# Attention and two mixture stages on one core: the steps of the heads issued in parts by engine, 79 of the parts placed by a table, and the sums and scales of the values kept in another PSUM bank

## Chip, cores and metric

The program runs on one core of one Trainium2 chip. The metric is the time of one execution on the device in microseconds (us). The profiled execution has a span, from the first to the last instruction, and a time of its own that also holds what lies around the span.

## What is computed

An attention over 2 batches of 8 heads (768 positions, head size 64), in which a query sees the keys that have the same signs under a random projection; its output goes through a dense layer pair and then through a layer pair chosen by token.

```python
mask = q_bucket[:, :, :, None] == k_bucket[:, :, None, :]
scores = np.where(mask, scale * np.matmul(q, k.transpose(0, 1, 3, 2)), -1000000000.0)
...
attn = attn / (np.sum(attn, axis=-1, keepdims=True) + 1e-09)
x = np.matmul(attn, v)              # then rows of 512 for 1536 tokens
x = (s * np.maximum(x @ w_in, 0) ** 2 + b) @ w_out
out[mask_e] = gate * (np.maximum(x[mask_e] @ w1[e], 0) @ w2[e])   # e: the token's expert, 8 of them
```

## The kernel before

The attention takes heads 0 to 15 in pairs p. Its work is a list of events, each with a key of 10 times a block number plus a priority; a program sorts the list by key and then calls the events one after the other. A call issues all of an event's instructions, so the key sets the order on every engine at once, and each engine works through its own instructions in that order. Block 6h+j belongs to head h and key block j (768 keys are 6 blocks of 128). Events of the start have negative keys.

The events of a head are these. `trans` (L193) turns q or k of a pair on TensorE and splits it in a high and a low part: `qh`, `kh` on ScalarE, `ql`, `kl` on VectorE. `bits` (L252 to L277) multiplies both with the projection, six pairs of matmuls into one PSUM tile, and VectorE writes the signs (`aux`). `asm` and `asm_aux` copy the parts by DMA into the operands `Q1`, `Q2`, `K1`, `K2` of a head. `maxp` (L383) multiplies for one block of queries; VectorE reduces the rows to the maximum (`mx`). `mops` (L394) makes four small VectorE operands of it, and `mrow` (L407, L416) puts them into a row of `Q1` by way of TensorE and ScalarE (`NM` is written last). `st` (L429) multiplies keys with queries, ScalarE takes the exponential `e` and for most blocks its half-precision part `eh`, and GpSimd makes the rest `el`. `avs` (L451) multiplies `e`, or `eh` and `el`, with the values, for half of the queries at a time, and `fin` (L478) divides.

The values are made ready beside that: `load_v` (a DMA from GpSimd's queue), `vabs` (ScalarE, a bound of their size), `vred` (GpSimd, sums over blocks, three additions `vt`, `vsm`, `vsm`), `vscan` (column sums by TensorE), `vscale0` to `vscale2` (a common scale for a group of pairs: VectorE, a transposition by TensorE, five tiny VectorE steps, a broadcast by TensorE, a copy `sc`), `vsums` (ScalarE `vr`, `vp`, then VectorE `vb`), `vxs`, `vx`, `vxl` (values scaled and split) and `vsel` (GpSimd `VS`). There are three such groups: pair 0, pairs 1 to 3, pairs 4 to 7.

PSUM has three tiles of two banks for everything of `trans`, `bits`, `maxp`, `mrow`, `st`, `xt` and, before the change, also for `vscale1`, `vscale2` and `vscan` of the later groups (`self.ps`, tag S). Who needs a tile waits on the engine that read its last content. Two more banks, `av0` and `av1`, hold the sums of `avs` for even and odd heads. `warm` issues matmuls on zeros in the start. Heads 0 to 3 have their `maxp` inside the blocks of the heads before.

Of the kernel before, what the change touches and what calls it, by code (L numbers as in the profile page):

```python
# [20 lines left out]
HALF = 384  # L21
# [7 lines left out]
XN = [[f"x{g}{i}" for i in "hl"] for g in range(3)]  # L29
AT = dict(vx=-2, tq=-20, tk=-19, bits=-17, mo=-6, mr=2, xt=21, mx=-12, vs=4,  # L30
# [11 lines left out]
class Attn:  # L42
    def __init__(self, ctx, natctx, hlctx, qkctx, qkctx2, tc, psS, psA, ident, identb, q, k, v, proj, xt, x1, x2):
# [55 lines left out]
        self.vps = {}  # L99

# [93 lines left out]
    def trans(self, p, nm):  # L194
        nc = self.nc
        a = self.qt[p][nm]
        ps = self.ps("trans")
        for j in range(NB):
            nc.tensor.matmul(out=ps[:, j // 3, (j % 3) * 128:(j % 3) * 128 + 128], lhsT=a[:, j].rearrange("p h d -> p (h d)"), rhs=self.ident,
                             is_transpose=True)  # L200
        hl = self.hl if p % 2 else self.hl0
        hi = hl.tile([128, S], F32R, tag=nm + "h", name=nm + "h")
        lo = hl.tile([128, S], F32R, tag=nm + "l", name=nm + "l")
        nc.scalar.activation(out=h2(hi), in_=ps[:, :, 0:HALF], func=ACTF.Copy)
        nc.vector.tensor_tensor(out=h2(lo), in0=ps[:, :, 0:HALF], in1=h2(f(hi)), op=ALU.subtract)
        self.qt[p][nm + "h"] = hi
        self.qt[p][nm + "l"] = lo

    def asm(self, h, nm, parts=(0, 1)):
        p, r = divmod(h, 2)  # L210
        t = self.qt[p]
        rows = slice(64 * r, 64 * r + 64)
        i = h % 4
        dma = lambda out, in_: self.nc.sync.dma_start(out=f(out), in_=f(in_))
        hi, lo = t[nm + "h"][rows], t[nm + "l"][rows]
        if nm == "q":
            if 0 in parts:
# [34 lines left out]
    def bits(self, p):  # L252
        self.bits1(p)
        self.bits2(p)

    def bits1(self, p):
# [7 lines left out]
        t["bps"] = ps  # L264

    def bits2(self, p):
        nc = self.nc
        t = self.qt[p]
        ps = t.pop("bps")
        if p == 0:  # L270
            for o, out, m in ((32, self.Q1[1], 1.0), (96, self.K1[1], -PEN)):
                nc.vector.tensor_scalar(out=h2(out[64:76]), in0=ps[o:o + 12, :, 0:HALF], scalar1=self.thr[o:o + 12, 0:1], scalar2=m,
                                        op0=ALU.is_gt, op1=ALU.mult)
            return
        aux = (self.hl if p % 2 else self.hl0).tile([128, S], F32R, tag="aux", name="aux")
        nc.vector.tensor_scalar(out=h2(aux), in0=ps[:, :, 0:HALF], scalar1=self.thr[:, 0:1], scalar2=self.thr[:, 1:2],
                                op0=ALU.is_gt, op1=ALU.mult)  # L277
        t["aux"] = aux

    def bits0(self, nm):  # L280
# [16 lines left out]
    def vred(self, p):  # L297
# [4 lines left out]
        add(x, vn[:, :, 0:3], vn[:, :, 3:6])  # L302
        add(o, x[:, :, 0], x[:, :, 1])
        add(o, o, x[:, :, 2])

    def vscan(self, lo, hi):

        nc = self.nc
        if lo:
            self.vps = self.ps("vsum")[:, 0]  # L310
            for p in range(lo, hi):
                nc.tensor.matmul(out=self.vps[0:12, (p % 4) * 128:(p % 4) * 128 + 128].rearrange("p (h d) -> p h d", h=2),
                                 lhsT=self.one[:, 0:12], rhs=self.vsm[:, p % 4])
            return
        self.vps = self.psA.tile([128, 512], F32, tag="av1", name="vsum")
        for j in range(NB):
            nc.tensor.matmul(out=self.vps[0:12, 0:128].rearrange("p (h d) -> p h d", h=2), lhsT=self.one[:, 0:12], rhs=self.vn[0][:, :, j],
# [9 lines left out]
    def vscale0(self, i):  # L327
        self.vsr = self.sm.tile([128, 4], F32, tag="vr", name="vr", bufs=1)
        self.nc.vector.tensor_reduce(out=self.vsr[:, 3:4], in_=self.vm[:, (0, 1, 4)[i]:(1, 4, 8)[i]], axis=AX.X, op=ALU.max)
# [13 lines left out]
    def vscale2(self, i):  # L343
        ps = self.ps("vscale")[:, 0]
        self.nc.tensor.matmul(out=ps[:, 0:3], lhsT=self.one[0:1], rhs=self.vsr[0:1, 0:3])
        self.nc.vector.tensor_copy(self.sc[i], ps[:, 0:3])

    def vsums(self, lo, hi):
# [34 lines left out]
    def maxp(self, h, j):  # L383
# [23 lines left out]
    def mrow0(self, h):  # L407
# [4 lines left out]
        nc.tensor.matmul(out=ps[:, 0, HALF:512], lhsT=self.MP[h % 2], rhs=self.identb)  # L412
        nc.scalar.activation(out=h2(self.Q1[h][96:98]), in_=ps[96:98, :, 0:HALF], func=ACTF.Copy)
        nc.scalar.activation(out=self.NM[h % 3][0:12], in_=ps[0:12, 0, HALF:512], func=ACTF.Copy)

    def mrow(self, h):  # L416
        if h < 4:
            return self.mrow0(h)
# [3 lines left out]
        nc.tensor.matmul(out=ps[:, 0:128], lhsT=MP, rhs=self.identb)  # L422
        r1 = self.sm.tile([64, 128], F32R, tag="mr1", name="mr1")
        nc.scalar.activation(out=r1[32:44], in_=ps[32:44, 0:128], func=ACTF.Copy)
        nc.scalar.activation(out=self.NM[h % 3][0:12], in_=ps[0:12, 0:128], func=ACTF.Copy)
        for c in range(2):
            nc.sync.dma_start(out=f(self.Q1[h % 4][96 + c:97 + c]).rearrange("c (j q) -> c j q", j=NB), in_=f(r1[32 + 6 * c:38 + 6 * c]))

    def st(self, h, j):  # L429
# [16 lines left out]
        self.E[h, j] = (eh, el)
# [41 lines left out]
    def xt(self, p):  # L488
# [9 lines left out]
        elif p < self.NP - 1:  # L498
            return self.xt_parts(p, xn)
# [4 lines left out]
        for i, (j0, j1) in enumerate(parts):  # L504
            for j in range(j0, j1):
                nc.tensor.matmul(out=ps[i][:, (j - j0) * 128:(j - j0) * 128 + 128], lhsT=xn[:, j], rhs=self.ident, is_transpose=True)
        dst = []
        for i, (j0, j1) in enumerate(parts):
# [23 lines left out]

    def program(self, extra):

        ev = []

        def at(g, pri, fn, *a):
            ev.append((10 * g + pri, len(ev), fn, a))
# [30 lines left out]
        pre(self.bits1, 0)  # L569
# [7 lines left out]
        pre(self.bits2, 0)  # L577
# [5 lines left out]
        pre(self.vscale1)  # L583
# [12 lines left out]
        at(8, 0, self.vscale1)  # L596
# [8 lines left out]
        at(22, 0, self.vscale1)  # L605
# [52 lines left out]
        return [(e[0] // 10, (lambda e=e: e[2](*e[3]))) for e in ev]  # L658
# [777 lines left out]
def fused_kernel(tc, q, k, v, proj, w_in, w_out, s, b, ids, w_gate, mbias, w1, w2, out):  # L1436
    nc = tc.nc
    with ExitStack() as c:
# [29 lines left out]
        with tc.manual_schedule():  # L1468
# [41 lines left out]

            def close_attn():
# [8 lines left out]
            M.program(open_route, lambda: A.xt(7), close_attn, end1)  # L1520
# [56 lines left out]
```

## Time and profile before

| | |
|---|---|
| median of 3 runs | 723.19 us (722.99 to 725.15) |
| the profiled execution's own time | 723.74 us |
| its span | 721.9 us |
| busy: TensorE (PE) / its weight loads | 682.7 / 597.2 us |
| busy: VectorE (DVE) / ScalarE (ACT) / GpSimd (POOL) | 424.2 / 368.2 / 233.7 us |

The attention takes the first 280 us, the dense layers the stretch up to about 530 us, the expert layers the rest. A busy share says little by itself: it is read by stretch, and where an engine is idle, by what ended the wait.

### The profile page before, as it was taken

To read this page: it belongs to the slowest core of one execution; us is meant where nothing else is said; L and a number is where in the kernel's file an instruction comes from. 1 tells how busy PE (TensorE), PEld (TensorE's weight loads), DVE (VectorE), ACT (ScalarE), POOL (GpSimd) and SP (SyncE) were. 2 spreads that over 40 slices of the span, in tenths; PEclk is the share of its full clock that TensorE was granted. 3 is DMA by queue.
4 is the path that set the end of the run, shared out by engine and by line. 5 is a ranking of instruction groups with operands and counts; after the bars stand their busy time and mean duration, and the time that the engine had idled before them with its cause. 6 is when DMAs were issued, how large, how long until landed. Compare 5 with 4: busy or idle time off the path is not lost.

```text
span 721.9 us, 12814 instructions
## 1 busy us (share of the span) xinstructions
PE 682.7 (95%) x5003; PEld 597.2 (83%) x5003; DVE 424.2 (59%) x825; ACT 368.2 (51%) x579; POOL 233.7 (32%) x244
## 2 busy tenths in 40 slices
PE   8789899999999989999999999999999899999993
PEld 5577789899887878788888888888889789999993
DVE  5745767676668677788874432245663775545411
ACT  5565777876867875555452232232352154344412
POOL 7576776867876740000000000200010114040112
PEclk9998999999999999999999999999999999999998
DMA  9399435456364132343420010001431356435201
GB/s 198 94 193 220 99 79 115 109 117 146 74 168 121 32 108 73 115 145 116 125 81 0 1 45 15 1 30 38 145 127 45 120 166 200 134 120 162 70 18 46
DMA packets 52998, 72.33 MB, mean 100 GB/s; under 512 B 30320, under 2 KB 30832, under 8 KB 52928
## 3 DMA queue, kind: packets, MB, share of 16 engines
q1 hardware_dynamic: 49808, 62.24, 32.3%
q0 software_dynamic: 2960, 9.18, 4.1%
q8 instruction: 41, 0.67, 0.4%
q14 instruction: 29, 0.24, 0.1%
q10 hardware_dynamic: 160, 0.00, 0.0%
HBM read 46.31 MB, written 6.42 MB: 73 GB/s over the span
## 4 chain that ended last, share of the span: by engine, by line
PE 66%; ACT 9%; issue 8%; DVE 7%; POOL 6%; DMA 2%; SPq 1%; POOLq 0%; DVEq 0%; ACTq 0%
PE Y L958 17%; PE H L900 16%; PE H L1250 7%; PE Y L1270 7%; PE Sst L436 5%; PE av L457 5%; ACT e L438 4%; PE Sbits L263 2%; PE Smaxp L390 2%; POOL el L445 2%; ACT eh L444 2%; PE mlr L988 1%; DVE mx L392 1%; PE mxt L1237 1%; DMA xg<-yd,ix 1%
## 5 line engine op out<-in xcount | busy, mean ns | idle before, releaser
L445 POOL TENSOR_TENSOR el<-e,eh 128x768 f16<-128x768 f32 x78 | 128.3, 1650 | 72.6 <-ACT eh L444 60.2
L958 PE MATMUL Y<-gh,W 128*128 128x512 f32 x384 | 128.8, 393 | 0.5 <-DVE sv L968 0.5
L392 DVE TENSOR_REDUCE mx<-Smaxp 128x1 f32<-128x768 f32 x96 | 90.2, 952 | 38.7 <-PE Smaxp L390 38.3
L438 ACT ACTIVATE e<-Sst 128x768 f32<-128x768 f32 x96 | 77.1, 803 | 46.7 <-PE Sst L436 42.7
L436 PE MATMUL Sst<-Q,K 128*128 128x384 f32 x384 | 91.6, 360 | 1.9 <-ACT e L438 1.6
L958 PEld LDWEIGHTS Y<-gh,W 128*128 128x128 f32 x384 | 72.1, 188 | 15.6 <-DVE sv L968 0.9
L1270 PE MATMUL Y<-hh,W 128*128 128x400 f32 x256 | 80.0, 354 | 0.0
L958 PE MATMUL Y<-gl,W 128*128 128x512 f32 x192 | 74.8, 390 | 0.0
L913 DVE SCALAR_TENSOR_TENSOR r<-r,sb 128x512 f32<-128x512 f32 x46 | 35.8, 777 | 62.2 <-ACT r L912 62.1
L436 PEld LDWEIGHTS Sst<-Q,K 128*128 128x128 f32 x384 | 63.3, 190 | 5.9 <-ACT e L438 2.8
L444 ACT ACTIVATE eh<-e 128x768 f16<-128x768 f32 x78 | 65.8, 844 | 2.5
L912 ACT ACTIVATE r<-H 128x512 f32<-128x512 f32 x44 | 26.3, 597 | 78.5 <-PE H L900 78.5
L886 POOL IOTA ev<- 128x96 f32 x1 | 0.3, 299 | 190.4 <-PE H L900 190.4
L920 ACT ACTIVATE gh<-r,sb 128x512 fp32r<-128x512 f32 x46 | 33.2, 725 | 53.0 <-PE Y L958 53.0
L390 PE MATMUL Smaxp<-K,Q 96*128 96x384 f32 x192 | 50.9, 351 | 9.5 <-ACT e L438 3.9
L1223 POOL DMA_INDIRECT xg<-yd,ix x16 | 17.5, 1092 | 121.3 <-DVE nf L1209 117.7
L921 DVE SCALAR_TENSOR_TENSOR gl<-r,sb,gh 128x512 fp32r<-128x512 f32 x46 | 34.4, 749 | 34.2 <-ACT gh L920 34.0
L457 PE MATMUL av<-VX,eh 128*128 128x65 f16 (+1 forms) x936 | 50.3, 195 | 0.4 <-POOL VX L381 0.4
L457 PEld LDWEIGHTS <-eh 128*128 128x128 f16 x936 | 38.6, 99 | 13.7 <-issue 13.1
L1157 DVE TENSOR_TENSOR W<-st,W 128x1024 fp32r<-128x1024 f32 x32 | 38.8, 1222 | 17.6 <-ACT W L1156 17.6
L1270 PEld LDWEIGHTS Y<-hh,W 128*128 128x128 f32 x256 | 47.7, 188 | 0.0
L390 PEld LDWEIGHTS Smaxp<-K,Q 96*128 96x128 f32 x192 | 34.0, 191 | 15.3 <-ACT e L438 6.1
(349 smaller groups left out, 1469.4 us busy)
## 6 DMA issues: line engine op xcount, KB each, us to landing
st<-in_moe_w_dram SPq DMA_DIRECT2D x32, 512.0 KB
sw<-in_moe_w_in_dram SPq DMA_DIRECT2D x16, 512.0 KB
sw<-in_moe_w_out_dram SPq DMA_DIRECT2D x16, 512.0 KB
Q<-qh SPq DMA_DIRECT2D x30, 192.0 KB
K<-kh SPq DMA_DIRECT2D x30, 192.0 KB
nq<-in_q_dram SPq DMA_DIRECT2D x16, 192.0 KB
nk<-in_k_dram SPq DMA_DIRECT2D x16, 192.0 KB
yd<-row SPq DMA_DIRECT2D x12, 256.0 KB
```

Of the source, the lines that this page charges most:

```text
L390: nc.tensor.matmul(out=ps[:, a, 0:HALF], lhsT=self.Q1[i][0:96, j * 128:j * 128 + 128], rhs=self.K1[i][0:96, a * HALF:a * HALF + HALF])
L392: nc.vector.tensor_reduce(out=self.mx[h][:, j:j + 1], in_=ps[:, :, 0:HALF], axis=AX.XY, op=ALU.max)
L436: nc.tensor.matmul(out=ps[:, a, 0:HALF], lhsT=K[:, c], rhs=Q[:, a * HALF:a * HALF + HALF], start=(n == 0), stop=(n == 1))
L438: nc.scalar.activation(out=h2(e), in_=ps[:, :, 0:HALF], func=ACTF.Exp, scale=0.125)
L444: nc.scalar.activation(out=eh, in_=e, func=ACTF.Copy)
L445: nc.gpsimd.tensor_tensor(out=el, in0=e, in1=eh, op=ALU.subtract)
L457: mm = lambda q, n, e, v, start=False, stop=False: nc.tensor.matmul(out=av[:, q, 0:n], lhsT=e, rhs=v, start=start, stop=stop, skip_group_c ...
L900: self.nc.tensor.matmul(out=ps, lhsT=w[:, k, fs], rhs=x[:, k], start=(k == 0 and n == 0), stop=(k == 3 and n == 2))
L958: nc.tensor.matmul(out=self.yp[d], lhsT=w[:, i, ds], rhs=x, start=(fc in (0, FA) and n == 0), stop=(fc in (FA - 1, 15) and n == 2))
L1157: nc.vector.tensor_tensor(out=lo[:, o], in0=d["st"], in1=f(hi[:, o]), op=ALU.subtract)
L1250: nc.tensor.matmul(out=ps, lhsT=w, rhs=xx[:, kd, 0:C], start=(n == 0), stop=(n == 11))
L1270: nc.tensor.matmul(out=self.yp[d][:, 0:C], lhsT=w, rhs=xx, start=(fc == 0 and n == 0), stop=(fc == 7 and n == 2))
```

## The change

Each event that uses several engines becomes a generator with a `yield` between the work of one engine and the next. `at` puts each part into the list as an event of its own, with the event's key, unless the table `MOVED` holds another key for it (79 parts). The projection of `bits` is cut four times more, inside its matmuls. `vscan`, `vscale1` and `vscale2` write to one tile `vps` in an `av` bank that no head uses at that time, in place of tiles of tag S. For pair 0 the first maximum (`vscale0`) is left out, as there is one column. `load_v` of pairs 1 and 2 is issued in the start.

```diff
+MOVED = {
+    "bits:0/0": -800.5029, "bits:0/1": -796.5039, "vscale0:0/0": -751.9531, "load_v:1/0": -744.375, "vscan:0,1/0": -657.5391,
...
+    "maxp:2,3/0": 76.75, "st:1,0/3": 77.9531, "bits:2/0": 78.9062, "trans:2,k/0": 83, "maxp:2,4/1": 85.2812,
...
     def maxp(self, h, j):
...
+        yield
         nc.vector.tensor_reduce(out=self.mx[h][:, j:j + 1], in_=ps[:, :, 0:HALF], axis=AX.XY, op=ALU.max)
...
+    def vtile(self, i):
+        if self.vps.get("i") != i:
+            self.vps = {"i": i, "t": self.psA.tile([128, 512], F32, tag=f"av{i == 0:d}", name="vps")}
+        return self.vps["t"]
...
-    def vscale1(self):
+    def vscale1(self, i):
         nc, V = self.nc, self.nc.vector
-        ps = self.ps("vscale")[:, 0]
+        o = 128 * (i == 0)
+        ps = self.vtile(i)[0:1, o:o + 128]
         r = self.vsr
-        nc.tensor.matmul(out=ps[0:1, 0:128], lhsT=r[:, 3:4], rhs=self.ident, is_transpose=True)
-        V.tensor_reduce(out=r[0:1, 0:1], in_=ps[0:1, 0:128], axis=AX.X, op=ALU.max)
+        nc.tensor.matmul(out=ps, lhsT=self.vmx, rhs=self.ident, is_transpose=True)
+        yield
+        V.tensor_reduce(out=r[0:1, 0:1], in_=ps, axis=AX.X, op=ALU.max)
...
+    def parts(self, it, n=6):
+
+        done = [0]
+        self.running.append(it)
+
+        def step(i):
+            if done[0] == i:
+                done[0] += 1
+                next(it, None)
+
+        return [lambda i=i: step(i) for i in range(n)]
...
-            ev.append((10 * g + pri, len(ev), fn, a))
+            name = fn.__name__ + ":" + ",".join(str(x) for x in a if isinstance(x, (int, str, tuple)))
...
+            if inspect.isgeneratorfunction(fn):
+                steps = self.parts(fn(*a))
+            else:
+                steps = [lambda: fn(*a)]
+            for i, step in enumerate(steps):
+                ev.append((MOVED.get(f"{name}/{i}{tag}", 10 * g + pri), len(ev), step))
```

What the table does to the order is shown at three places. The first is TensorE at the end of the start and in the first block. Before (`Svscale` are the two matmuls of `vscale1` and `vscale2` of pair 0, `Sst` the scores of head 0, `Smaxp` those for the maxima of head 1):

```order
L317 MATMUL vsum<-tx0h,one 12x128 x6
L335 MATMUL Svscale<-iw,vr 1x128
L436 MATMUL Sst<-Q_0_126,K_0_127 128x384 x2
L436 MATMUL Sst<-Q_0_128,K_0_129 128x384 x2
L345 MATMUL Svscale<-vr,one 128x3
L199 MATMUL Strans<-iw,nq 128x128 x6
L436 MATMUL Sst<-Q_0_126,K_0_127 128x384 x2
L436 MATMUL Sst<-Q_0_128,K_0_129 128x384 x2
L390 MATMUL Smaxp<-K_1_131,Q_1_130 128x384 x4
L199 MATMUL Strans<-iw,nk 128x128 x6
```

The same place of the change:

```order
L269 MATMUL wps<-dm 128x512
L365 MATMUL vps<-iw,vm 1x128
L477 MATMUL Sst<-Q_0_126,K_0_127 128x384 x2
L477 MATMUL Sst<-Q_0_128,K_0_129 128x384 x2
L425 MATMUL Smaxp<-K_1_131,Q_1_130 128x384 x4
L377 MATMUL vps<-vr,one 128x3
L219 MATMUL Strans<-iw,nq 128x128 x6
L477 MATMUL Sst<-Q_0_126,K_0_127 128x384 x2
L477 MATMUL Sst<-Q_0_128,K_0_129 128x384 x2
L219 MATMUL Strans<-iw,nk 128x128 x6
```

The sums `vsum` have gone further up, among the matmuls on zeros; the two `maxp` of head 1 stand before the broadcast of the scale, which waits for VectorE, and the small matmuls write to `vps`.

The second place is TensorE at the end of head 0 and in the first blocks of head 1, where q of pair 2 is turned and the scale of pairs 1 to 3 is made. Before:

```order
L457 MATMUL av_491<-VS_148,NM_150 128x65
L199 MATMUL Strans<-iw,nq 128x128 x6
L335 MATMUL Svscale<-iw,vr 1x128
L436 MATMUL Sst<-Q_1_130,K_1_131 128x384 x2
L436 MATMUL Sst<-Q_1_132,K_1_133 128x384 x2
L390 MATMUL Smaxp<-K_2_135,Q_2_134 128x384 x4
L457 LDWEIGHTS eh
```

The change, from the last matmuls of head 0 on (ahead of them it has `Strans<-iw,nq` and one `Smaxp` between the two halves of `avs`):

```order
L501 MATMUL av_489<-VS_148,NM_150 128x65
L286 MATMUL Sbits<-qh,WQ_122 128x384 x2
L286 MATMUL Sbits<-qh,WQ_123 128x384 x2
L477 MATMUL Sst<-Q_1_130,K_1_131 128x384 x2
L477 MATMUL Sst<-Q_1_132,K_1_133 128x384 x2
L425 MATMUL Smaxp<-K_2_135,Q_2_134 128x384 x2
L219 MATMUL Strans<-iw,nk 128x128 x6
L365 MATMUL vps<-iw,vr 1x128
L501 LDWEIGHTS eh
```

`vscale1` stands seven rows further down, behind `st`, a `maxp` and the turning of k; the first third of `bits` has come up in front of `st`.

The third place is GpSimd's queue in the blocks of head 0. Before (`DMA ...<-in_v_dram` are `load_v` of pairs 2 and 3):

```order
L180 DMA tx2h<-in_v_dram 128x2x384
L445 TENSOR_TENSOR el<-e,eh 128x768 x2
L180 DMA tx2h<-in_v_dram 128x2x384
L301 TENSOR_TENSOR vt<-tx0h 128x384
L301 TENSOR_TENSOR vsm<-vt 128x128
L301 TENSOR_TENSOR vsm<-vsm,vt 128x128
L365 TENSOR_TENSOR VS_148<-vb_157,msk 12x792
L445 TENSOR_TENSOR el<-e,eh 128x768
```

The change:

```order
L322 TENSOR_TENSOR vt<-tx0h 128x384
L416 TENSOR_TENSOR VX_144<-tx0h,VX_144 128x5x64
L490 TENSOR_TENSOR el<-e,eh 128x768 x2
L416 TENSOR_TENSOR VX_144<-tx0h,VX_144 128x5x64
L490 TENSOR_TENSOR el<-e,eh 128x768
L200 DMA tx2h<-in_v_dram 128x2x384
L322 TENSOR_TENSOR vsm<-vt 128x128
L322 TENSOR_TENSOR vsm<-vsm,vt 128x128
L399 TENSOR_TENSOR VS_148<-vb_157,msk 12x792
L490 TENSOR_TENSOR el<-e,eh 128x768
```

`vt` of pair 1 has moved up by six instructions, the loads of pairs 1 and 2 are gone from here into the start, and `VS` stands before the last `el` of head 0.

## Rows read from the trace of the kernel before

**Rows 1.** Windows by stretch: length; busy us of PE, PEld, DVE, ACT, POOL; clock, DMA.

```profile
24.00:41.00 17.00, 13.44 (x121) 10.76 (x119) 12.17 (x23) 11.13 (x17) 10.90 (x10) 1.00 0.58 139
41.00:58.00 17.00, 14.12 (x130) 12.83 (x128) 8.49 (x17) 10.23 (x16) 15.73 (x18) 0.90 0.95 203
58.00:70.00 12.00, 10.41 (x96) 8.40 (x94) 5.88 (x13) 7.14 (x11) 6.52 (x8) 0.86 0.92 221
...
99.00:200.00 101.00, 99.12 (x1174) 90.47 (x1175) 69.34 (x118) 77.76 (x113) 76.29 (x57) 1.00 0.52 113
...
280.00:477.00 197.00, 196.51 (x886) 162.96 (x885) 116.13 (x199) 79.95 (x135) 4.31 (x18) 1.00 0.20 62
```

**Rows 2.** Timeline of PE in the start: start, length, instruction, idle time before it.

```profile
13.18 0.93 PE L390 MATMUL Smaxp<-K,Q 96*128 96x384 f32 x4 [1.27 <-DVE K L290]
13.96 0.86 PE L263 MATMUL Sbits<-qh,WQ 128*128 128x384 f32 x4
...
21.02 0.49 PE L411 MATMUL Smrow<-identb,tx0l 128*128 128x128 bf16 x6 [0.60 <-DVE tx0l L405]
...
22.36 1.48 PE L317 MATMUL vsum<-tx0h,one 128*12 128x128 f32 x12
```

**Rows 3.** Timeline of PE in the first blocks of head 0.

```profile
27.91 0.61 PE L390 MATMUL Smaxp<-K,Q 96*128 96x384 f32 x2 [0.56 <-ACT e L438]
...
31.87 0.61 PE L390 MATMUL Smaxp<-K,Q 96*128 96x384 f32 x2 [1.32 <-ACT e L438]
...
32.96 0.31 PE L457 MATMUL av<-VX,eh 128*128 128x64 f16 x5 [0.42 <-POOL VX L381]
```

**Rows 4.** Timeline of PE from the end of head 0 on.

```profile
47.37 0.25 PE L457 MATMUL av<-VS,NM 128*128 128x65 f16 x3 [0.58 <-POOL VS L365]
...
51.14 0.27 PE L335 MATMUL Svscale<-iw,vr 128*1 128x128 f32 x1 [2.05 <-DVE vr L329]
```

**Rows 5.** Windows: granted clock (1.00 is 2.4 GHz) after the five busy times.

```profile
52.50:55.90 3.40, 3.40 (x29) 3.17 (x28) 2.69 (x5) 2.25 (x3) 3.07 (x3) 0.50 1.12 256
...
62.80:66.20 3.40, 1.95 (x13) 1.19 (x10) 0.33 (x2) 3.36 (x7) 3.34 (x4) 1.00 0.77 211
66.20:69.60 3.40, 3.40 (x26) 3.10 (x27) 2.31 (x4) 0.62 (x2) 0.10 (x1) 0.50 0.99 215
79.80:83.30 3.50, 2.17 (x17) 1.69 (x17) 2.52 (x5) 2.76 (x4) 3.34 (x5) 1.00 0.00 0
```

**Rows 6.** Timeline of PE near the end of head 1.

```profile
64.52 0.62 PE L390 MATMUL Smaxp<-K,Q 96*128 96x384 f32 x2 [0.52 <-ACT NM L414]
66.07 0.93 PE L390 MATMUL Smaxp<-K,Q 96*128 96x384 f32 x2 [0.94 <-ACT vp L356]
```

**Rows 7.** Timeline of PE in heads 2 and 3.

```profile
81.08 0.88 PE L199 MATMUL Strans<-iw,nq 128*128 128x128 f32 x6 [1.34 <-DVE mx L392]
...
83.97 0.62 PE L390 MATMUL Smaxp<-K,Q 96*128 96x384 f32 x2 [0.71 <-ACT NM L414]
...
98.86 0.62 PE L390 MATMUL Smaxp<-K,Q 96*128 96x384 f32 x2 [1.09 <-ACT e L438]
```

**Rows 8.** The page, part 5: groups of el, mx and e, with the mean of one.

```profile
L445 POOL TENSOR_TENSOR el<-e,eh 128x768 f16<-128x768 f32 x78 | 128.3, 1650 | 72.6 <-ACT eh L444 60.2
...
L392 DVE TENSOR_REDUCE mx<-Smaxp 128x1 f32<-128x768 f32 x96 | 90.2, 952 | 38.7 <-PE Smaxp L390 38.3
L438 ACT ACTIVATE e<-Sst 128x768 f32<-128x768 f32 x96 | 77.1, 803 | 46.7 <-PE Sst L436 42.7
```

**Rows 9.** DVE and POOL together near the end of head 2, by timeline.

```profile
77.28 1.65 POOL L445 TENSOR_TENSOR el<-e,eh 128x768 f16<-128x768 f32 x1 [1.48 <-ACT eh L444]
77.63 1.32 DVE L400 TENSOR_SCALAR mc<-mx 128x6 f32<-128x6 f32 x1
```

**Rows 10.** The tile mc: shortest, median and longest in ns.

```profile
L400 DVE TENSOR_SCALAR mc<-mx x16: 159/161/1572, 20.2 to 245.9; 128x6 f32<-128x6 f32 x16
```

**Rows 11.** Issue and landing of loads of the values, by DMA issues.

```profile
tx2l<-in_v_dram POOLq DMA_DIRECT2D x2, 384.0 KB, 6.9
```

More of the change, by code (lines that the diff above doesn't have):

```diff
@@ L2 @@
 from collections import deque
+import inspect
 import math
@@ L99, in __init__ @@
         self.vps = {}
+        self.running = []
     def setup(self):
@@ L203, in trans @@
         lo = hl.tile([128, S], F32R, tag=nm + "l", name=nm + "l")
-        nc.scalar.activation(out=h2(hi), in_=ps[:, :, 0:HALF], func=ACTF.Copy)
-        nc.vector.tensor_tensor(out=h2(lo), in0=ps[:, :, 0:HALF], in1=h2(f(hi)), op=ALU.subtract)
         self.qt[p][nm + "h"] = hi
         self.qt[p][nm + "l"] = lo
+        nc.scalar.activation(out=h2(hi), in_=ps[:, :, 0:HALF], func=ACTF.Copy)
+        yield
+        nc.vector.tensor_tensor(out=h2(lo), in0=ps[:, :, 0:HALF], in1=h2(f(hi)), op=ALU.subtract)
     def asm(self, h, nm, parts=(0, 1)):
@@ L302, in vred @@
         add(x, vn[:, :, 0:3], vn[:, :, 3:6])
+        yield
         add(o, x[:, :, 0], x[:, :, 1])
         add(o, o, x[:, :, 2])
+    def vtile(self, i):
+        if self.vps.get("i") != i:
+            self.vps = {"i": i, "t": self.psA.tile([128, 512], F32, tag=f"av{i == 0:d}", name="vps")}
+        return self.vps["t"]
     def vscan(self, lo, hi):
         nc = self.nc
+        ps = self.vtile(self.group(lo))
         if lo:
-            self.vps = self.ps("vsum")[:, 0]
             for p in range(lo, hi):
-                nc.tensor.matmul(out=self.vps[0:12, (p % 4) * 128:(p % 4) * 128 + 128].rearrange("p (h d) -> p h d", h=2),
+                nc.tensor.matmul(out=ps[0:12, (p % 4) * 128:(p % 4) * 128 + 128].rearrange("p (h d) -> p h d", h=2),
                                  lhsT=self.one[:, 0:12], rhs=self.vsm[:, p % 4])
             return
-        self.vps = self.psA.tile([128, 512], F32, tag="av1", name="vsum")
         for j in range(NB):
-            nc.tensor.matmul(out=self.vps[0:12, 0:128].rearrange("p (h d) -> p h d", h=2), lhsT=self.one[:, 0:12], rhs=self.vn[0][:, :, j],
+            nc.tensor.matmul(out=ps[0:12, 0:128].rearrange("p (h d) -> p h d", h=2), lhsT=self.one[:, 0:12], rhs=self.vn[0][:, :, j],
                              start=(j == 0), stop=(j == NB - 1))
@@ L343, in vscale2 @@
     def vscale2(self, i):
-        ps = self.ps("vscale")[:, 0]
-        self.nc.tensor.matmul(out=ps[:, 0:3], lhsT=self.one[0:1], rhs=self.vsr[0:1, 0:3])
-        self.nc.vector.tensor_copy(self.sc[i], ps[:, 0:3])
+        o = 256 * (i == 0)
+        ps = self.vtile(i)[:, o:o + 3]
+        self.nc.tensor.matmul(out=ps, lhsT=self.one[0:1], rhs=self.vsr[0:1, 0:3])
+        yield
+        self.nc.vector.tensor_copy(self.sc[i], ps)
     def vsums(self, lo, hi):
@@ L417, in mrow @@
         if h < 4:
-            return self.mrow0(h)
+            yield from self.mrow0(h)
+            return
         nc = self.nc
@@ L498, in xt @@
         elif p < self.NP - 1:
-            return self.xt_parts(p, xn)
+            self.xt_parts(p, xn)
+            return
         else:
@@ L513, in xt, with xt_all @@
             dst.append((lo, ps[i][:, 0:n], hi))
+        yield
         for lo, src, hi in dst:
             nc.vector.tensor_tensor(out=lo, in0=src, in1=f(hi), op=ALU.subtract)
+    def xt_all(self, p):
+        deque(self.xt(p), 0)
     def xt_parts(self, p, xn):
@@ L568, in program @@
         pre(self.maxp, 0, 1)
-        pre(self.bits1, 0)
+        pre(self.bits, 0)
         pre(self.maxp, 0, 2)
@@ L582, in program @@
         pre(self.vscan, 0, 1)
-        pre(self.vscale1)
+        pre(self.vscale1, 0)
         at(0, 2, self.vscale2, 0)
@@ L595, in program @@
         at(7, 9, self.vscale0, 1)
-        at(8, 0, self.vscale1)
+        at(8, 5, self.vscale1, 1)
         at(9, 4, self.vscale2, 1)
@@ L604, in program @@
         at(20, 9, self.vscale0, 2)
-        at(22, 0, self.vscale1)
+        at(22, 0, self.vscale1, 2)
         at(23, 4, self.vscale2, 2)
@@ L657, in program @@
         ev.sort(key=lambda e: e[:2])
-        return [(e[0] // 10, (lambda e=e: e[2](*e[3]))) for e in ev]
+        return [(int(e[0] // 10), e[2]) for e in ev]
 C = 400
@@ L1509, in fused_kernel @@
                 fn()
+            assert not any(it.gi_frame for it in A.running)
             def close_attn():
```

45 lines of the change are left out of this document (32 added, 13 removed), and 14 rows, old and new, of the table MOVED.

## The prediction

> **What bounds the kernel now.** I read the windows by stretch first. From 99 to 200 us TensorE is busy 99.12 us of 101, and in the dense layers 196.51 of 197 [rows 1]: there the order of other engines can give nothing, and whatever is gained ahead of it shifts all that follows. The changed order lies ahead of it. From 24 to 70 us TensorE is idle for 3.56, 2.88 and 1.59 us of three stretches (17.00 less 13.44, 17.00 less 14.12, 12.00 less 10.41) [rows 1], though no other engine is full: in 41 to 58 us GpSimd has 15.73 busy us of 17, and the issue of its loads comes on top. So no engine bounds this part; single waits in TensorE's queue do, and the timeline of TensorE names each with what ended it. The reader is to see three kinds: a tile of tag S not yet read (ended by `e` or `mx`), a result of a side chain that stands in line too early (`vr`, `VS`, `VX`), and ScalarE's queue being late (`NM`, `vp`).
>
> The clock is a second loss. TensorE ran at 1.2 GHz, half its rate, from 52.5 to 55.9 us and from 66.2 to 69.6 us [rows 5], each time just behind a stretch with long waits: 0.58 and 2.05 us [rows 4], and 0.52 and 0.94 us [rows 6]. Each spell of 3.4 us at half rate costs some 1.7 us of work.
>
> **The change, part by part.** I go through TensorE's new queue by hand, with the durations of these rows, and ask at each step which wait is left.
>
> Start, 13 to 24 us. TensorE waits 1.27 us for the signs of k of head 0 and 0.60 us for `mops` [rows 2]. The change puts the first three of six pairs of `bits` (pairs of 0.86 us per two, pipelined) into the first wait, and the `vsum` (1.48 us) ahead of the second. Both waits are covered by work that was to be done anyway; VectorE's six reductions then run back to back, so `mops` comes about 1 us earlier. What is left is a short wait of `st` for ScalarE's row copy, some 0.3 us. Gain 1.87 - 0.3, about **1.5 us**.
>
> Blocks 0 to 4, 24 to 41 us, idle 3.56 us. The wait for the scale's tiny steps goes (two `maxp` stand ahead of it), that for `VX` (0.42 us) too, as ScalarE makes `VX` ahead of `eh` and GpSimd's loads have left its queue. But `st` of block 1 now needs the tile of `maxp` of head 1, behind a reduction of 0.95 us [rows 8], some 0.7 us; and the longest wait here, 1.32 us for `e` of block 2 [rows 3], stays: ahead of that `e`, ScalarE's queue still holds `VX`, an `eh` and `kh`, each about as long as the `e` of 0.80 us [rows 8]. I keep 1.6 us for it and 0.3 us for the rest, 2.6 in all. Gain **1.0 us**.
>
> End of head 0, 41 to 58 us, idle 2.88 us. `VS` (0.58 us) is made some microseconds earlier, since `vt` and two load issues have left the queue ahead of it. `vscale1` waits no longer 2.05 us [rows 4]: `st`, two `maxp`, the turning of k and a third of `bits` go first, some 3 us of work. What it waits for is new: its bank is that of head 0, so it needs `fin` of head 0. Behind it stand the first `avs` of head 1. `fin` comes behind `ql`, the maximum of the bounds and one reduction on VectorE; by the durations it ends some 0.4 us before TensorE arrives. Waits of 0.15 to 0.3 us stay at four places where `bits`, `st`, `maxp` and `trans` follow closely on the engine that they need; I keep 1.0 us. Gain 1.9 us, and 1.7 us for the first spell at half rate. Together **3.6 us**.
>
> End of head 1, 58 to 70 us, idle 1.59 us. `vr` and `vp` no longer hold a tile of tag S, so the wait of 0.94 us [rows 6] goes. But they now stand ahead of the row copy and `NM` on ScalarE, which is busy 3.36 of 3.40 us there [rows 5], and the second `maxp` needs `NM`. I keep 0.8 us. Gain 0.8 us, and 1.7 us for the second spell. Together **2.5 us**.
>
> Heads 2 and 3, 79 to 99 us. Three waits, 1.34, 0.71 and 1.09 us [rows 7], 3.14 in all. `trans` of pair 3 goes ahead of the `maxp` that meet the late reduction, `trans` of k between `st` and the `maxp` that waits for `NM` (its 0.6 us fills most of 0.71), and the last wait came from a fourth user of the three tiles, `vscale1`, which has left them. I keep 1.4 us. Gain **1.7 us**.
>
> The sum is 1.5 + 1.0 + 3.6 + 2.5 + 1.7 = 10.3 us. The instructions are the same but for one reduction less. The two loads go out in the start, where GpSimd's queue has nothing to do until the first `el`; `vt` of pair 1, which now stands ahead of the first `VX` part, needs its load some 12 us later, against 6.9 us to land [rows 11]. The `el` that have gone behind `vred` in heads 0 to 2 end, by my count, a microsecond or more before the `avs` that read them; on the DMA queue of SP one copy for head 4 goes some rows back, long before its reader.
>
> One thing speaks against taking it whole. VectorE's small `mc` takes 0.16 us as a rule and up to 1.57 [rows 10]; the long one at 77.63 us ended with the `el` that GpSimd had begun at 77.28 [rows 9]. The Trainium skill (SBUF — State Buffer, section "Who interferes with whom") says why: VectorE and GpSimd share a pair of SBUF ports, which one instruction holds to its end while the other blocks. That would agree with this row; by it the change, which leaves GpSimd fewer gaps, would block more often and my sum would stand at its lower bound. In rows alone: `mc`, `vb` and their like stand in line for TensorE in three `mops`, so between nothing and three times 1.4 us (1.57 - 0.16) is lost, 4.2 us. Since GpSimd was busy 15.73 of 17 us already before the stretch is shortened, I take the middle, 2 us.
>
> 10.3 - 2.0 = 8.3 us off the profiled 723.74 us is 715.4. The median stands 0.55 us below the profiled time, which gives **715 us**.
>
> **Rivals.** *The other engines take back half.* In the shortened stretch GpSimd must do the same 33 us of work (10.90 + 15.73 + 6.52 in 24 to 70 us, and its load issues) in some 38 us, and the DMA queues, at 0.95 and 0.92 of their time [rows 1], the same bytes: 203 GB/s for 17 us and 221 for 12 are 6.1 MB, in 21 us 290 GB/s, above the 256 of the fullest window here [rows 5]. Some of these bytes aren't urgent (loads for blocks much later), and two loads have left. Against it: the operands of head 4 have some 4 us to spare by my count. For it: a load of the values took 6.9 us to land [rows 11]. If blocking costs all 4.2 us and late operands 2 us, 4.1 us are gained: about **719 us**.
>
> *Slower, by the clock.* The waits that I keep are smaller but many. 1.45 us idle of 3.40 [rows 5] led to a spell at half rate; 1.33 of 3.50 did not [rows 5]. The two kept waits of 0.7 and 1.6 us in blocks 0 to 4 lie as near to each other. The Trainium skill (TensorE: Matmul & The Clock Gate, Part 1, "The HAM clock gate") states that half rate is the resting state and that activity lifts it; the rows agree as far as each spell follows waits. Each new spell costs 1.7 us. One is likely enough to be within my range; the kernel is slower by 0.3% only if six or seven more appear than I count (8.3 and 2.2 us by 1.7), that is, if most of 24 to 46 us runs at 1.2 GHz: **726 us**.
>
> *Nothing changes in the end.* If GpSimd and ScalarE, not the order, already set the pace of 24 to 99 us, waits would only move. ScalarE at 11.13 of 17 and 10.23 of 17 us speaks against it: **723 us**.
>
> *More than I take.* If the kept waits are half of my count (3.0 of 0.3 + 2.6 + 1.0 + 0.8 + 1.4 = 6.1 us) and no blocking is added, 13 us are gained: **710 us**.
>
> **How the numbers follow.** Forecast, 712 to 718: 0.50. Half taken back, 718 to 721: 0.22. More gained, under 712: 0.13. No change: 0.08. Slower: 0.07. A measurement of this kernel can tell about 0.3%, 2.2 us, from no change. Faster by that (below 721.0) is then 0.50 + 0.22 + 0.13, of which I leave 0.02 to the edge: 0.83; the same 0.10; slower 0.07. The range reaches from the case of more gain to the edge of the half taken back: 710.5 to 720.5, with 0.10 below and above 0.13 at most left out.
>
> **What would show it.** Right: no wait for `vr` ahead of `vscale1` and none for `VS` or `vp`; granted clock 1.00 through 24 to 99 us; the first `st` at about 22.3 us, the first `st` of head 2 some 7 us earlier than now; the dense layers of the same length, shifted. Wrong: a spell at half rate in 24 to 40 us; TensorE waiting at `vscale1` for `fin`; `maxp` of head 4 waiting for a DMA; `mc` at 1 us or more in several heads; or a stretch behind 99 us that grows by what the front gained.

## The result, and the profile after

| | before | after |
|---|---|---|
| median | 723.64 us (722.42 to 725.15, 8 runs) | 716.6 us (714.38 to 721.24, 8 runs) |
| ratio, 95% interval | 1 | 0.9903 [0.9878, 0.9928] |
| profiled execution: time, span | 723.74, 721.9 us | 716.97, 715.1 us |

The forecast was 715.0 us in 710.5 to 720.5. Five rows of TensorE's timeline of the kernel before, not shown so far, serve as marks: the first `st` of heads 0, 1 and 2 and the last matmul of `mrow` of heads 5 and 12.

```profile
23.80 0.94 PE L436 MATMUL Sst<-Q,K 128*128 128x384 f32 x4
...
42.33 0.96 PE L436 MATMUL Sst<-Q,K 128*128 128x384 f32 x4
...
67.82 0.99 PE L436 MATMUL Sst<-Q,K 128*128 128x384 f32 x2
...
109.54 0.22 PE L422 MATMUL Smrow<-identb,MP 128*128 128x128 bf16 x1
...
207.81 0.22 PE L422 MATMUL Smrow<-identb,MP 128*128 128x128 bf16 x1
```

The same timeline of the changed kernel, with its marks and its longer waits (in brackets: the idle time ahead and what the profile names for it).

```profile
13.02 0.94 PE L425 MATMUL Smaxp<-K,Q 96*128 96x384 f32 x4 [0.21 <-DVE K L311]
...
22.05 0.98 PE L477 MATMUL Sst<-Q,K 128*128 128x384 f32 x4
...
29.98 0.62 PE L425 MATMUL Smaxp<-K,Q 96*128 96x384 f32 x2 [1.44 <-ACT e L480]
...
38.71 0.95 PE L477 MATMUL Sst<-Q,K 128*128 128x384 f32 x4
40.83 0.59 PE L425 MATMUL Smaxp<-K,Q 96*128 96x384 f32 x2 [1.16 <-DMA K<-aux]
...
48.70 0.88 PE L219 MATMUL Strans<-iw,nk 128*128 128x128 f32 x6 [0.40 <-ACT e L480]
49.42 0.27 PE L365 MATMUL vps<-iw,vr 128*1 128x128 f32 x1
...
58.43 0.62 PE L425 MATMUL Smaxp<-K,Q 96*128 96x384 f32 x2 [0.45 <-ACT NM L452]
...
61.99 1.32 PE L477 MATMUL Sst<-Q,K 128*128 128x384 f32 x4 [2.38 <-DMA Q<-ql]
...
90.88 0.97 PE L477 MATMUL Sst<-Q,K 128*128 128x384 f32 x4 [0.21 <-ACT e L480]
...
100.06 0.22 PE L461 MATMUL Smrow<-identb,MP 128*128 128x128 bf16 x1
...
196.85 0.22 PE L461 MATMUL Smrow<-identb,MP 128*128 128x128 bf16 x1
```

The marks moved up by 1.75, 3.62, 5.83, 9.5 and 11.0 us. Of the waits of [rows 2], [rows 4] and [rows 7] next to nothing is left: `vscale1` (49.42) runs straight behind the turning of k, and from 79 to 99 us one wait of 0.21 us stands. Of [rows 6] the wait for `vp` is gone; the one for `NM` stays, 0.45 us at 58.43 where it was 0.52. But two waits are there that the kernel before didn't have: 1.16 us at 40.83 (before, that place had 0.25 us) and 2.38 us at 61.99, the first `st` of head 2.

The windows of the changed kernel, with the columns of [rows 1] and [rows 5]:

```profile
24.00:41.00 17.00, 13.49 (x137) 11.32 (x137) 11.96 (x18) 13.88 (x22) 15.71 (x15) 1.00 0.52 124
41.00:58.00 17.00, 16.56 (x166) 14.02 (x165) 12.32 (x25) 11.55 (x17) 13.70 (x16) 1.00 1.01 227
58.00:70.00 12.00, 9.19 (x80) 8.44 (x80) 8.42 (x9) 6.85 (x12) 7.17 (x7) 0.86 1.02 221
79.00:99.00 20.00, 19.79 (x219) 17.91 (x217) 13.85 (x32) 16.28 (x26) 16.82 (x17) 1.00 0.51 111
280.00:477.00 197.00, 196.51 (x892) 163.14 (x891) 112.91 (x200) 77.95 (x133) 4.31 (x18) 1.00 0.20 62
...
58.90:62.30 3.40, 1.02 (x21) 0.90 (x21) 3.01 (x4) 0.80 (x2) 2.96 (x4) 1.00 0.95 250
62.30:65.75 3.45, 3.45 (x20) 3.14 (x19) 1.76 (x2) 1.65 (x2) 0.64 (x1) 0.52 0.98 243
...
243.30:246.60 3.30, 1.60 (x23) 1.20 (x23) 2.64 (x4) 2.81 (x5) 2.69 (x2) 1.00 0.51 142
246.70:250.10 3.40, 3.40 (x26) 2.78 (x26) 2.56 (x5) 1.83 (x3) 0.77 (x1) 0.50 0.30 58
553.90:557.30 3.40, 1.92 (x17) 1.50 (x16) 3.12 (x16) 0.51 (x1) 0.00 (x0) 1.00 0.00 0
557.30:560.70 3.40, 3.40 (x26) 2.70 (x25) 2.06 (x9) 0.00 (x0) 0.00 (x0) 0.51 0.00 0
```

The spell at half rate at 52.5 us is gone (1.00 in 41 to 58 us, against 0.90). The second one came again, at 62.3 us, right behind the new wait: TensorE had been busy for 1.02 us of 3.40. Two more stand at 246.7 and 557.3 us, each behind a stretch in which TensorE was busy for about half of the time. The dense layers are unchanged.

**Which engine made the new waits?** The row at 61.99 names a transfer, Q from `ql`. That transfer was issued at about 30 us. TensorE's weight load of the same `st` names something else:

```profile
61.99 0.81 PEld L477 LDWEIGHTS Sst<-Q,K 128*128 128x128 f32 x4 [2.50 <-DVE mx L428]
```

VectorE and GpSimd in the changed kernel, by timeline, ahead of both waits:

```profile
34.19 1.23 DVE L436 TENSOR_SCALAR mc<-mx 128x6 f32<-128x6 f32 x1
...
36.22 1.07 DVE L295 TENSOR_SCALAR aux<-Sbits,thr 128x768 fp32r<-128x768 f32 x1
...
59.04 2.87 DVE L393 TENSOR_SCALAR vb<-msk 12x6 f16<-12x6 f32 x1
59.11 2.80 DVE L428 TENSOR_REDUCE mx<-Smaxp 128x1 f32<-128x768 f32 x2
```

```profile
33.75 1.65 POOL L490 TENSOR_TENSOR el<-e,eh 128x768 f16<-128x768 f32 x1 [0.49 <-ACT eh L487]
...
58.65 0.76 POOL L200 DMA_DIRECT2D nv<-in_v_dram  x1
59.44 0.78 POOL L416 TENSOR_TENSOR VX<-tx0h,VX 128x320 f16<-128x320 f32 x1
60.16 1.00 POOL L322 TENSOR_TENSOR vt<-tx2l 128x384 f32<-128x384 f32 x1
61.11 0.77 POOL L416 TENSOR_TENSOR VX<-tx0h,VX 128x320 f16<-128x320 f32 x1
```

The ones column of `vb`, 12 x 6 values, ended at 61.91 us, and GpSimd's row of three instructions (`VX`, `vt`, `VX`) at 61.88. In the kernel before the same step takes 0.16 us. The `mx` that `st` needs stands behind it: two `mx` began at 59.11 and 59.98 us, and their ends are recorded with the column's, at 61.91. `mc` of head 1 likewise ended at 35.42 us with an `el` that ended at 35.40; `aux`, which the changed order puts behind it, left late, and so did the transfers that `maxp` at 40.83 waited for. This is a reading; the experiments test it.

### The profile page after: what moved, and what is told of

Read it like the earlier page. It is cut to its first block, busy times and chain, and to the rows that moved or that the text cites. A ratio compares the mean times of both kernels' runs of the same rounds, so it can differ in the third digit from the quotient of the medians.

```text
span 715.1 us, 12814 instructions
## 1 busy us (share of the span) xinstructions
PE 681.3 (95%) x5003; PEld 597.1 (84%) x5003; DVE 424.2 (59%) x824; ACT 369.1 (52%) x579; POOL 233.8 (33%) x244
## 4 chain that ended last, share of the span: by engine, by line
PE 74%; ACT 8%; issue 7%; DVE 5%; POOL 3%; DMA 2%; SPq 0%; POOLq 0%; ACTq 0%; DVEq 0%
PE Y L1028 17%; PE H L970 16%; PE H L1320 8%; PE Sst L477 7%; PE Y L1340 7%; PE av L501 6%; ACT e L480 4%; PE Smaxp L425 3%; PE Sbits L286 2%; PE mlr L1058 1%; ACT eh L487 1%; PE Strans L219 1%; PE lH L970 1%; PE mxt L1307 1%; DMA xg<-yd,ix 1%
## 5 line engine op out<-in xcount | busy, mean ns | idle before, releaser
L1327 ACT ACTIVATE hh<-H 128x400 fp32r<-128x400 f32 x32 | 16.0, 501 | 55.1 <-PE Y L1340 46.4
```

## Experiments

The theory: VectorE's small steps on operands in SBUF are held while GpSimd works, and hand this on to TensorE. The rival that the row at 61.99 suggests: late operand transfers, as the DMA share is 1.02 in 58 to 70 us. A further question is whether the table, the bank or the splitting made the gain.

**The table empty.** All 79 entries are taken out.

```diff
-MOVED = { ... 79 entries ... }
+MOVED = {}
```

> The table of moved parts is empty; the split into parts and the bank for the sums and scales of the values stay. By the theory of the prediction (the order brings most) what is left is the waits for vr, vp and the last e of heads 2 and 3 that the bank takes away, some 2 to 3 us and at most one half-rate spell of 1.7 us: 719 to 721 us against 723.6 before. By the rival that the bank brings nearly all: 717 us, as in the changed kernel. By the rival that splitting and the bank bring nothing without the table: 723 us.

728.19 us (727.17 to 732.78), 1.0056 [1.0038, 1.0073] of before: slower than before, which no theory had. Its timeline of TensorE, from the slowest of its runs (732.78 us):

```profile
23.25 0.49 PE L430 MATMUL Smrow<-identb,tx0l 128*128 128x128 bf16 x6 [1.40 <-DVE tx0l L424]
...
55.97 0.37 PE L348 MATMUL vps<-iw,vr 128*1 128x128 f32 x1 [2.13 <-DVE xn L512]
```

The start is 2.2 us later than before (`mrow` at 23.25, before at 21.02 [rows 2]), since the writing of the signs of pair 0 (16.82 to 18.89 us on VectorE), now a part of `bits`, stands ahead of four reductions and `mops` until the table moves it. And `vscale1` does wait for `fin` (which writes `xn`), 2.13 us in place of the 2.05 us for `vr`: what the prediction feared of the bank is real, and the moved order alone hides it. So splitting and bank together bring no gain by themselves; the two were not taken apart here.

**The table for the front alone.** The entries of parts with old keys of 50 and more are taken out.

```diff
 MOVED = {
     ...  24 entries, old keys below 50
-    "trans:2,q/0": 75.4531, ... , "trans:5,q/2": 414.9844,   (55 entries)
 }
```

> Only the 24 entries of the table whose parts stood ahead of key 50 (the start and blocks 0 to 4) stay. By the prediction's terms for the start and blocks 0 to 4 (1.5 + 1.0 us) it is 2.5 us below the kernel with an empty table, 717 to 718.5 us, and half-rate spells as before near 52 and 66 us may come back. By the rival that the changed kernel's gain lies in heads 0 to 3 it is no faster than the kernel with an empty table.

722.0 us (721.51 to 726.19), 0.9986 [0.997, 1.0003] of before, so not told apart from it. 6.2 us less than with the empty table, more than the 2.5 expected, since it also mends the start that the split had made later: the first `st` moves from 26.03 to 22.40 us, 3.6 us of it. The half-rate spells are back (clock 0.90 in 41 to 58 us, 0.87 in 58 to 70). About 5 us of the change's 7 come from the later entries.

**The ones column later.** It becomes a part of its own, moved behind the two reductions; in VectorE's queue it then stands behind two more, four in all.

```diff
+    "vsums:1,4/2": 125,
...
+        yield
         V.tensor_scalar(out=vb[:, hs, D:D + 1], in0=self.msk[:, 0:1].unsqueeze(1).to_broadcast([12, n, 1]),
```

> In the changed kernel TensorE waits 2.38 us at the first st of head 2. Two theories. GpSimd holds VectorE: the tiny step that writes the ones column of vb (0.17 us alone) took from 59.04 to 61.91 us, while GpSimd worked to 61.88 us, and the reduction that st needs stood behind it. Here that step goes behind two more reductions (key 125), so st should start at about 60.1 us instead of 61.99, and the half-rate spell behind it should go: 1.9 + 1.7 us less, about 713 us. Late operand: the transfer that the profile names (Q from ql) ends the wait; then nothing changes, 716.6 us and a wait of 2.4 us at that st.

711.92 us (711.36 to 712.83), 0.9832 [0.9816, 0.9848] of before; the interval lies clear of the changed kernel's. VectorE, then TensorE, by timeline:

```profile
59.29 1.80 DVE L429 TENSOR_REDUCE mx<-Smaxp 128x1 f32<-128x768 f32 x2
...
63.38 1.36 DVE L394 TENSOR_SCALAR vb<-msk 12x6 f16<-12x6 f32 x1
```

```profile
60.29 0.97 PE L478 MATMUL Sst<-Q,K 128*128 128x384 f32 x4 [0.43 <-DVE mx L429]
```

No transfer was touched, the wait fell from 2.38 to 0.43 us, and the half-rate spell behind it is gone (clock 1.00 in 58 to 70 us). The rival falls. Wait and spell make 3.7 of the 4.7 us gained (1.95 and 1.7); this profile also lacks the spell at 246.7 us. The two `mx` took 1.80 us, their usual length [rows 8], while GpSimd worked on `VX` and `vt` (59.69 to 61.43 us); the column, now at 63.38, is held again (1.36 us, until an `el`), and there nobody waits for it.

**The signs ahead of `mops`.** One entry is taken out.

```diff
-    "bits:1/4": 45.625,
```

> The signs of pair 1 (aux) go back ahead of mops of head 1 on VectorE. In the changed kernel mc of head 1 took 1.23 us from 34.19 us on, until an el of GpSimd ended at 35.40, aux went out behind it and its transfers ended TensorE's wait of 1.16 us at 40.83 us. By the theory that this wait is the blocked mc handed on: aux ends some 1.1 to 2.0 us earlier, the wait goes, mops ends no later than about 36.8 us, when TensorE needs it; about 1.0 us less, 715.5 us. By the rival that mrow of head 1 then waits for mops as long as it gained: 716.6 us.

715.29 us (714.2 to 715.59), 0.9873 [0.9855, 0.9891]. The wait of 1.16 us is gone and 0.27 us stands at `mrow` instead. The size is as expected, but by times alone, whose intervals overlap, it is not shown. The trace shows it up to head 2: from the first `st` of head 0 to that of head 2 it is 38.9 us (22.56 to 61.46), 39.94 in the changed kernel, 1.04 us less. Behind that the profiles differ by their spells: here one of twice the length (60.5 to 67.3 us) and none at 246.7 and 557.3.

**A gap on GpSimd's side.** The addition `vt` of pair 4 goes back behind the next three `el`.

```diff
-    "vred:4/0": 131.5,
```

> The other side of the blocked step: it stays where the changed kernel has it, and GpSimd gets a gap. The addition vt of pair 4, which stood between the two VX parts from 60.16 to 61.16 us, goes back to its own key (149), behind the first parts el of head 2. If the ones column of vb is held until GpSimd's unbroken row of work ends, that end moves from 61.88 to about 60.9 us, the step takes about 1.9 us in place of 2.87, and the wait at the first st of head 2 is 1.4 us in place of 2.38: 715.6 us, or 714 us if the half-rate spell behind it goes too. If GpSimd has nothing to do with it, the step and the wait keep their lengths: 716.6 us.

713.99 us (713.41 to 717.67), 0.9868 [0.9843, 0.9894]; by times alone the interval meets the changed kernel's. VectorE, GpSimd and TensorE by timeline:

```profile
59.17 1.93 DVE L393 TENSOR_SCALAR vb<-msk 12x6 f16<-12x6 f32 x1
```

```profile
59.57 1.50 POOL L416 TENSOR_TENSOR VX<-tx0h,VX 128x320 f16<-128x320 f32 x2
```

```profile
61.18 0.98 PE L477 MATMUL Sst<-Q,K 128*128 128x384 f32 x4 [1.44 <-DVE mx L428]
```

With one addition less in GpSimd's row, the column ends at 61.10 instead of 61.91 us, again with the row (61.07), and TensorE's wait is 1.44 us. Both lengths were forecast to within 0.05 us. VectorE's queue is the same as in the changed kernel, so GpSimd's side sets the length of the step. The spell behind the wait is gone too.

**No bank.** Sums and scales of the later groups in tiles of tag S, the table as it is.

```diff
+    def vnew(self, i):
+        if i:
+            self.vps = {"i": i, "t": self.ps("vps")[:, 0]}
+        return self.vtile(i)
...
-        ps = self.vtile(i)[0:1, o:o + 128]
+        ps = self.vnew(i)[0:1, o:o + 128]
```

> The table stays, but the sums and scales of the two later groups of values are kept in tiles of tag S again, as in the kernel before. By the prediction the bank is worth the wait for vp (0.94 us) and most of the last wait in heads 2 and 3 (1.09 us), 2 us: 718.5 us, and 720 us if a half-rate spell comes with it. By the reading of the kernel with an empty table, where a wait of 2.13 us for fin and one of 1.06 us stood in place of the 2.05 and 0.94 us, the bank is worth nothing by itself, and the time stays at 716 to 717 us.

713.42 us (711.44 to 718.52), 0.9861 [0.9832, 0.9891]: not slower than with the bank; that it is faster isn't shown, as the intervals overlap. TensorE, then VectorE, by timeline:

```profile
53.96 0.38 PE L384 MATMUL Svps<-vr,one 1*128 1x3 f32 x2 [0.61 <-ACT e L487]
```

```profile
59.75 0.35 DVE L400 TENSOR_SCALAR vb<-msk 12x6 f16<-12x6 f32 x1
```

The tiles of tag S cost a wait of 0.61 us, and no wait for `vp` came back. The small steps come later: the column ends at 60.10 us, as GpSimd's DMA issue ends (60.13) and before its next instruction begins (60.43), so it takes 0.35 us and the wait of 2.38 us isn't there. The bank shows no gain here; where the small steps fall weighs more.

**Both mends.** The edits of the third and the fourth experiment together.

> Both mends together: the ones column of vb later and the signs of pair 1 ahead of mops. The two waits stand 20 us apart, and if each is VectorE held by GpSimd at its own place, the gains add: 4.7 and 1.3 us off 716.6, 710.6 us. If the second wait only takes up slack that the first had left, it is 711.9 us, as with the column alone.

712.16 us (710.48 to 713.3), 0.9831 [0.9811, 0.9851]. By the medians the gains don't add. By the traces the second mend brings 1.0 us more up to the dense layers: their first `x1h` matmul starts at 278.1 us in the changed kernel, at 273.9 with the column alone, at 272.9 with both. (Of the first step, 4.2 us, 1.7 is the spell at 246.7 us, which the two kernels with mends don't have.) The runs with both mends spread more: the two at a mean clock of 0.995 took 710.48 and 711.07 us, the other three, at 0.990 to 0.993, 712.16 to 713.3. Whether the second mend still tells in the whole is open.

**`e` ahead of `kh`.** On top of both mends, one exchange in ScalarE's queue, for the 1.44 us at 29.98.

```diff
+    "trans:1,k/1": 21.5, "trans:1,k/2": 21.6, "st:0,2/2": 21.7, "st:0,2/3": 21.8,
```

> On top of both mends, ScalarE makes the exponential e of block 2 of head 0 ahead of kh of pair 1 (one exchange in its queue, nothing else). The longest wait left in blocks 0 to 4, 1.43 us, ended with that e, which stood behind kh (0.80 us alone). By the prediction's reading (the wait is ScalarE's queue ahead of e) it shrinks by about 0.7 us: 710 us. By the rival that kl and the reductions behind it on VectorE then come as much later, a wait of that size appears at the next maxp and the time stays.

716.34 us (715.1 to 718.58), 0.9892 [0.987, 0.9915]: 4.2 us lost. The wait of 1.43 shrank to 0.75 us, but 0.52 us for `kl` appeared, as the rival said; and something neither had foreseen, in VectorE's, GpSimd's and TensorE's timelines:

```profile
37.87 3.98 DVE L442 TENSOR_TENSOR tx1h<-mc,tx1h 128x6 bf16<-128x6 f32 x1
```

```profile
37.75 1.50 POOL L400 TENSOR_TENSOR VS<-vb,msk 12x792 f16<-12x792 f16 x1
39.22 1.63 POOL L491 TENSOR_TENSOR el<-e,eh 128x768 f16<-128x768 f32 x1
40.81 0.98 POOL L322 TENSOR_TENSOR vt<-tx2h 128x384 f32<-128x384 f32 x1
```

```profile
41.90 0.82 PE L448 MATMUL Smrow<-identb,tx1h 128*128 128x128 bf16 x6 [3.88 <-DVE tx1h L442]
```

`mops` of head 1 came some tenths of a us later, its last step, 0.19 us alone, began 0.12 us behind `VS` and was held through three instructions. In 41 to 58 us the clock fell to 0.80.

**A gap for `mops`.** The same kernel, with `VS` and two short sums behind the next `el`.

```diff
+    "vsel:0/0": 52, "vred:1/1": 53,
```

> The kernel with both mends and the exchange on ScalarE, with one more move, on GpSimd alone: VS of pair 0 and the two short sums vsm of pair 1 go behind the next el. In the run without this move the last tiny step of mops of head 1 (0.19 us alone) took from 37.87 to 41.85 us while GpSimd worked without a gap on VS, an el and vt to 41.79 us, and TensorE waited 3.88 us for it. Here GpSimd has nothing to do from about 36.8 to 38.6 us, so that step should take about 0.2 us, TensorE's wait should be about 0.3 us and the low clock behind it (0.80 in 41 to 58 us) should go: about 712.5 us, as without the exchange. By the rival that the exchange itself (kh and kl later) made the loss, the wait and 716.3 us stay.

712.58 us (712.05 to 715.77), 0.9853 [0.9831, 0.9876]. The step takes 0.19 us (36.67 to 36.86) and `mrow` doesn't wait. The exchange on ScalarE is the same in both kernels and was not to blame by itself: it moved the step into GpSimd's row. VectorE, here and further on:

```profile
36.67 0.19 DVE L442 TENSOR_TENSOR tx1h<-mc,tx1h 128x6 bf16<-128x6 f32 x1
...
53.41 1.64 DVE L442 TENSOR_TENSOR tx0l<-mc,tx0l 128x6 bf16<-128x6 f32 x1
```

Now the same step of the next `mops` is held, and `maxp` waits 1.16 us for `aux` behind it, at 61.66 us.

**No bank, both mends.** The bank's experiment with the edits of both mends.

> The table with the sums and scales in tiles of tag S again, and both mends. The signs of pair 1 ahead of mops took away a wait of 1.1 us that the kernel without the bank has too; the ones column cost it only 0.35 us, so moving it brings nothing more. 713.4 less 1.1 to 1.3: about 712.2 us, the same as the kernel with the bank and both mends (712.2). If the bank brings something of its own once the blocked steps are out of the way, this kernel is slower than that one, 713.4 us or more.

713.41 us (710.9 to 715.42), 0.9851 [0.9829, 0.9874]. The wait at 41 us is gone as expected, but the same step of the next `mops` takes 1.69 us here too, and `maxp` waits 0.87 us for `aux` at 56.54. By times the bank is neither shown to help nor to harm: the two intervals overlap. The profiles put the kernel without it 2.3 us behind the one with it at `mrow` of head 5 (98.60 against 96.31), 0.87 of it by this wait, and 1.3 us at the first `x1h` matmul (274.2 against 272.9).

## Why the prediction was right

**Start:** gain 1.5 forecast, 1.75 measured (first `st` at 22.05; 22.3 was named). The waits of 1.27 and 0.60 us are covered, as said. One profile doesn't fix this closer than half a us: in the nine experiments that keep the table's order of the start, the first `st` stands at 21.7 to 22.7 us.

**Blocks 0 to 4:** 1.0 forecast; 3.62 less 1.75, 1.87 us, by the next mark. The waits that the text kept are there: 0.53 us for `mx` of block 1 (0.7), 1.44 us for `e` of block 2 (1.6).

**End of heads 0 and 1:** 1.9 and 0.8 us forecast, and 3.4 us for two spells; by the marks 5.83 less 3.62, 2.2 us, with the first spell gone and the two new waits, 3.5 us, inside. Two signs that the prediction named for being right did not come: the clock was 0.86 in 58 to 70 us, and the first `st` of head 2 came 5.8 us earlier in place of some 7. The waits for `VS`, `vr` and `vp` went, and `fin` didn't hold `vscale1`. That the bank took away the wait for `vp` was the wrong reason: without the bank it doesn't come back. Of the two half-rate spells one went (1.7 us, right), the other only changed its cause.

**Heads 2 and 3:** gain 1.7 forecast with 1.4 us of waits kept; 0.21 us is left of 3.14, a gain of 2.9. The mark behind them moved by 3.65 us more (9.48 less 5.83).

**GpSimd against VectorE:** this step failed in size. 2.0 us were taken out of 0 to 4.2, three times the loss of the longest `mc`. Measured are waits of 1.16 and 2.38 us, 3.5 together and still within it, and 1.7 for the spell behind the second: 5.2 us, outside its bounds. The price of a step was wrong: the prediction named `vb` beside `mc`, but took the longest `mc`, 1.57 us [rows 10], for the most that any of them can lose (the one of [rows 9], held by one `el`, took 1.32), and the column of `vb` lost 2.7. A step can be held through a row of GpSimd's instructions, and what stands behind it pays. The kernel before shows such a row already, just behind the `mc` of [rows 9]:

```profile
78.99 0.96 DVE L404 CAST tx1h<-mc 128x6 bf16<-128x6 f32 x1
```

```profile
78.89 1.03 POOL L301 TENSOR_TENSOR vt<-tx2l 128x384 f32<-128x384 f32 x1
```

A later step of the same `mops`, 0.18 us alone, was held by the `vt` behind the `el`, so one `mops` lost 1.9 us there (1.16 and 0.78), more than the 1.4 of the bound. In the changed kernel `mc` itself reached 1 us once in this stretch, 1.23 us in head 1; the one of 1.57 us in head 15 was there before. The Trainium skill (SBUF — State Buffer, section "Who interferes with whom") says that whichever of the two engines issues first keeps the shared ports for its whole instruction, and that on this chip a reduction on VectorE never contends for them. The 1.80 us for two `mx` next to GpSimd's `VX` and `vt` agree; the 2.87 and 3.98 us, which ended with the third instruction of GpSimd in a row, go beyond one instruction.

**The sum:** 8.3 us forecast, 9.5 measured behind heads 2 and 3 (`mrow` of head 5: 109.54 before, 100.06 after), and two errors in it nearly cancel: 5.2 us went to VectorE and the clock behind it instead of 2.0, and so some 14.7 us (9.5 + 5.2) were gained by the order instead of 10.3. That is a sum and not a measurement: with both mends, where 0.27 and 0.42 us of those waits are left and no spell, the same mark stands at 96.31 us, 13.2 us ahead of before. At `mrow` of head 12 it is 11.0 us. Behind that, gain is given back: the first `x1h` matmul of the dense layers starts 8.3 us earlier (286.4 before, 278.1 after), and the span is 6.8 us shorter. The spells at 246.7 and 557.3 us, which the kernel before doesn't have in its profile, make 1.7 us each of these 4.2. By the traces the rest lies at one place behind `mrow` of head 12, before and after:

```profile
209.49 0.62 PE L390 MATMUL Smaxp<-K,Q 96*128 96x384 f32 x2 [0.48 <-ACT NM L425]
```

```profile
198.52 0.97 PE L477 MATMUL Sst<-Q,K 128*128 128x384 f32 x4 [1.46 <-ACT NM L465]
```

TensorE waits 1.0 us longer for the same `NM`. The kernel with both mends has this wait too (1.45 us), the one without the bank but with the same order of instructions on every engine waits 0.43 us there; why was not tested. So the total is right, but partly by chance. The rival "the other engines take back half" had the right engine in GpSimd and the wrong one in the DMA: at a DMA share of 1.01 no operand came late except `aux`, which was sent late.

## What to carry to other kernels

Where a wait's row names an engine or transfer that was done long before, read the row of the weight load and the queue of the engine behind it; here it led from a transfer to a step of 72 values. When an order leaves GpSimd no gaps, look at every small VectorE step on SBUF operands that stands ahead of something TensorE needs: move it behind that, or leave a gap there. Price such a step by the row of GpSimd's instructions that it can meet, not by one; and expect each further change of order to bring another step into such a row.

## What was not expected of the hardware

- A VectorE step of 0.16 to 0.19 us took 2.87 and 3.98 us, to the end of three GpSimd instructions in a row; `mx`, which reads PSUM, kept its 0.9 us beside `VX` and `vt` where the column stood behind it.
- Half-rate spells are not the same in all runs. Those at 246.7 and 557.3 us follow on stretches with TensorE busy for 1.60 us of 3.30 and 1.92 of 3.40; the kernel before was busy for 1.70 us of 3.40 from 251.6 us and 2.01 of 3.50 from 562.0, and stayed at 2.4 GHz behind both in its profile. These spells are probably most of the spread of the runs: the changed kernel's fastest run, 714.38 us, had a mean clock of 0.991, its slowest, 721.24 us, 0.984, and 0.7% of 716 us is 5 of the 6.9 us between them. More was not tested.
